# A long convolution and two gated layers on one core: second-batch loads behind the words that are read, weight pieces decoded in halves, first weights loaded behind the last chunk

## The chip, the cores and the metric

The kernel runs on one core of one Trainium2 chip. The metric is the device time of one execution in microseconds (us). The core has a matrix engine (PE, TensorE), VectorE (DVE), ScalarE (ACT), GpSimd (POOL), and a queue (SP, SyncE) that issues all of this kernel's DMAs, which 16 DMA engines carry out.

## What is computed

Two batches of 3008 tokens with 256 channels pass a convolution over the whole sequence (by Fourier transform), and then two layers on each token. The first gates by silu and is 1536 wide, the second gates by a hard swish and is 2048 wide.

```
X = np.fft.rfft(x, axis=1)
Y = X * (filt_r + 1j * filt_i)[None, :, :]
y = np.fft.irfft(Y, n=x.shape[1], axis=1)         # (2, 3008, 256)
g = x @ w_gate; silu = g / (1 + exp(-g))          # x: y as 6016 tokens; 256 -> 1536
x = silu * (x @ w_val) @ w_out                    # 1536 -> 256
h = x @ w_in                                      # 256 -> 2048
out = (h * clip(h + 3, 0, 6) / 6) @ w_out2        # 2048 -> 256
```

The weights are float64. The kernel reads them as pairs of 32-bit words and makes a float32 value of each pair (it *decodes* them); that value is then split into a high and a low part for the matmuls.

## The kernel before

**Prologue.** The sequence of 3008 is 47 x 64, and the transform is made in two stages. Stage one of batch 0 (`time_to_slots`) makes 32 frequency slots and stores them to memory (`d1`). The **chunk stage** (lines 539 to 572, `i` from 0 to 18) then goes over 17 chunks of one or two slots. PE multiplies chunk `i` (L543); VectorE multiplies it with the filter (`filter_product`: L198, L200, L201, and a sum L149, which POOL does and for the last three chunks VectorE); two rounds later PE transforms back (`back`, L524), ScalarE copies the result to `qall` (L525), and SP stores a part of it to `d2` (L526). SP loads chunk `i + 4` (L460) and its filter (L469). The last two chunks (15 and 16) also go straight into the first block: `straight` (L535) multiplies them with the matrix `direct`, which is loaded into `late_mat`. The other slots come back from `d2` into `near` (`load_near`, L515): 16 slots, then 13, for the first block (`near[:, :4]`), and later all 32 for the second (`near[:, 4:]`).

**Weights.** `Decode` loads raw words (L243) and decodes in three parts: `start` (ScalarE's absolute value, L248), `leading` (VectorE, three instructions on the high word, L256, L257, L259) and `rest` (L266, L267 on the low word, and an add, L149, on POOL unless VectorE is named). `word` is `leading` and `rest`. `parts_w1` splits the result: ScalarE casts the high part, POOL makes the difference (L146). The first layer's weights come in 12 pieces `f` of 128 hidden units. The first two are loaded apart: gate and value parts by `load_gv` (words in `side`), the output parts of both as `both`. From piece 2 on `decode_w1` uses two places in `x0` in turn. The two places of `load_gv`'s words in `side` overlap: `side[:, 2560:3584]` holds the words of piece 1 and also the first two units of the second batch (`x1_unit`, loaded by `load_x1`, L502).

**Main loop** (from line 672). A step `t` multiplies one block of 512 tokens with one piece: gate and value, 12 matmuls (`l1`, L310). ScalarE's silu (L729) and VectorE's product (L751) make the hidden values `h`. Two steps are a pair `p`. In the first 12 pairs blocks 0 and 1 are taken in turn, so steps 0 to 3 use pieces 0 and 1, steps 4 to 7 pieces 2 and 3, steps 8 to 11 pieces 4 and 5. In each odd step PE also runs layer two of the pair before (`l2_plain`, 12 matmuls, L158); for that, ScalarE casts `h` to `hs` (L153) and VectorE makes its low part (L146). Step 1 also transforms `near[:, 4:]` into `xsd[1]` (L224), and a step of a pair brings units of the second batch through stage one (`staged`, L165).

The order of instructions on each engine is that of the program. SP keeps eight DMAs under way: each one that it issues waits until the one eight places before it has landed.

Of the kernel before, what the change touches and what calls it, by code (L numbers as in the profile page):

```python
# [20 lines left out]
NS = 32  # L21
# [6 lines left out]
DIRECT = 3  # L28
# [85 lines left out]
def fft_conv_glu_mlp(ctx: ExitStack, tc: tile.TileContext, x, filt, mats, direct, sgn, w1, w2, out):  # L114
    nc = tc.nc
    w1, w2 = w1.bitcast(U32), w2.bitcast(U32)
    n_chunk = len(CHUNKS)
# [24 lines left out]
    def bank(tag="gv"):  # L142
        return ps.tile([P, 512], F32, tag=tag, name=tag)
# [28 lines left out]
    def alone(i):  # L172

        return int(i == 0)
# [5 lines left out]
    def prepare_filter(i, ft, by_slot=False, both=True, top=0):  # L180

        s0, n = CHUNKS[i]
        o = slice(top, top + 64)
        if both:
            nc.scalar.copy(out=ft[64 - top:128 - top, :n, 0], in_=ft[o, :n, 0])
        if by_slot:
            for r in range(n):
                nc.scalar.mul(out=ft[o, r, 1], in_=ft[o, r, 1], mul=sg[o, s0 + r:s0 + r + 1])
            return
        nc.gpsimd.tensor_tensor(out=ft[o, :n, 1], in0=ft[o, :n, 1],  # L190
                                in1=sg[o, s0:s0 + n].unsqueeze(2).to_broadcast([64, n, D]), op=ALU.mult)

    def filter_product(i, acc, ft, u, t2, engine=nc.gpsimd, top=0):

        n = CHUNKS[i][1]
        o = slice(top, top + 64)
        xa = acc[:, :n * D].rearrange("p (s c) -> p s c", c=D)
        nc.vector.scalar_tensor_tensor(out=t2[0:64, :n], in0=xa[64:128], scalar=-1.0, in1=ft[o, :n, 1],  # L198
                                       op0=ALU.mult, op1=ALU.mult)
        nc.vector.tensor_tensor(out=t2[64:128, :n], in0=xa[0:64], in1=ft[o, :n, 1], op=ALU.mult)  # L200
        nc.vector.tensor_tensor(out=u[:, :n], in0=xa, in1=ft[:, :n, 0], op=ALU.mult)  # L201
        plus(u[:, :n], u[:, :n], t2[:, :n], engine)
        return u.rearrange("p s c -> p (s c)")[:, :n * D]
# [70 lines left out]
    def decode_w1(f):  # L274
        a = x0[:, f % 2 * 3072:][:, :3072]
        return Decode(None, w1[:, f, :], 768, (words(a[:, :1536]), a[:, 1536:2304], a[:, 2304:]))
# [9 lines left out]
    def parts_w1(d, f, engine=nc.gpsimd):  # L286
        parts_gv(d, f, engine)
        parts_o1(d, f, engine)
# [14 lines left out]
    def ntok(k):  # L303
        return BLOCKS[blocks[k][1]][1] * N2
# [112 lines left out]
    with tc.manual_schedule():  # L417
# [30 lines left out]
        def idle(n, cols):  # L448

            acc = bank()  # L450
            for _ in range(n):
                nc.tensor.matmul(acc[:, :cols], mat[:, 0, :], mat.rearrange("p a c -> p (a c)")[:, :cols])
# [4 lines left out]
        def load_chunk(i):  # L457
            s0, n = CHUNKS[i]
            bts[i] = x0[:96, 4096 + i % 4 * 512:][:, :n * D]
            nc.sync.dma_start(out=bts[i].rearrange("p (s c) -> p s c", c=D), in_=rows(d1[0], s0, n))  # L460

        def top(i):

            return i % 2 * 64

        def load_filter(i):
            s0, n = CHUNKS[i]
            fts[i] = x0[:, i % 4 * 1024:][:, :n * 2 * D].rearrange("p (s r c) -> p s r c", r=2, c=D)
            nc.sync.dma_start(out=fts[i][top(i):top(i) + N1P], in_=filt[0:N1P, s0:s0 + n])  # L469
# [9 lines left out]
        def words(a):  # L479
            return a.bitcast(U32).rearrange("p (n t) -> p n t", t=2)  # L480

        dec = {}

        def load_gv(f):
            a = (new_y if f == 0 else lambda: work.tile([P, 1024], F32, tag="g", name="g", bufs=1))()
            dec[f] = Decode(None, w1[:, f, :1024], 512, (words(side[:, 2560 * f:][:, :1024]), a[:, :512], a[:, 512:]))
# [14 lines left out]
        def load_x1(u):  # L501
            nc.sync.dma_start(out=x1_unit(u), in_=x[1, :, u * 512:(u + 1) * 512])  # L502
# [8 lines left out]
        def load_near(a, b, k=0):  # L511

            m = slice(4 * k, 4 * k + 4)
            for r in range(a, P, NS):
                nc.sync.dma_start(out=near[r:r + b - a, m],  # L515
                                  in_=d2[0].rearrange("m p c -> p m c")[r:r + b - a, m])
# [3 lines left out]
        def back(q):  # L520

            s0, n = CHUNKS[q]
            acc = bank("a")
            nc.tensor.matmul(acc[:96, :n * D], mat[:, 3 + alone(q), :96], ys[q])  # L524
            nc.scalar.copy(out=qall[:96, s0 * D:(s0 + n) * D], in_=acc[:96, :n * D])  # L525
            nc.sync.dma_start(out=rows(d2[0], s0, n)[0:32], in_=qs[0:32, s0:s0 + n])  # L526

        def straight(q):

            s0, n = CHUNKS[q]  # L530
            if not sums:
                sums.extend([bank("a"), bank("a")])
            for a in range(2):
                for r in range(n):
                    nc.tensor.matmul(sums[a], ys[q][:, r * D + a * P:r * D + (a + 1) * P],  # L535
                                     late_mat[:, s0 + r - NS + DIRECT],
                                     start=s0 + r == NS - DIRECT, stop=False)

        for i in range(n_chunk + 2):
            if i < n_chunk:  # L540
                n = CHUNKS[i][1]
                acc = bank()
                nc.tensor.matmul(acc[:, :n * D], mat[:96, 1 + alone(i), :], bts.pop(i))  # L543
                if i < 4:
                    idle(1, 384)
                if i % 2 == 0:
                    us = mlp.tile([P, 2, 2, 2, D], F32, tag="h", name="us")
                ys[i] = filter_product(i, acc, fts.pop(i), us[:, 0, i % 2], us[:, 1, i % 2],
                                       nc.vector if i >= n_chunk - 3 else nc.gpsimd, top(i))
                if i + 4 < n_chunk:  # L550
                    load_chunk(i + 4)
                    load_filter(i + 4)
                if i in (7, 10):
                    load_gv(i // 10)
                if i == 12:
                    nc.sync.dma_start(out=late_mat, in_=direct)
            if i in (n_chunk - 2, n_chunk - 1):
                dec[i - n_chunk + 2].start()
            q = i - 2
            if 0 <= q < n_chunk - 2:  # L560
                back(q)
                del ys[q]
            if q == n_chunk - 2:
                straight(q)
                a = x0[:, 4608:]
                both = Decode(None, w1[:, 0:2, 1024:], 512, (words(a[:, :1024]), a[:, 1024:], dec[0].a))
                load_near(16, NS - DIRECT)
                for f in (2, 3):
                    dec[f] = decode_w1(f)
                both.start()  # L570
            if q == 11:
                load_near(0, 16)
            if i + 3 < n_chunk:
                prepare_filter(i + 3, fts[i + 3], i % 2 == 1 or i + 5 == n_chunk, top=top(i + 3))
        straight(n_chunk - 1)

        def high_gv(f):
            nc.scalar.copy(out=wgv[:, f, 0], in_=dec[f].w)  # L578
# [14 lines left out]
            back(q)  # L593
        ys.clear()
        load_near(0, NS, 1)
        for u in range(2):
            load_x1(u)
        dec[1].rest(nc.vector)
        high_gv(1)
        both.leading()  # L600
        low_gv(1)
# [70 lines left out]
        for t in range(2 * n_pair):  # L672
            p, i = divmod(t, 2)
            k, g_ = steps[p]
            n, f, c = ntok(k), 2 * g_ + i, p - FIRST
# [52 lines left out]
            h = hid[p].chunk(i)  # L728
            nc.scalar.activation(out=h, in_=hid[p].halves(gate), func=AF.Silu)  # L729

            d = 2 if t == 2 else p + 2 if i == 0 and p > 1 else None
            if d in dec:
                parts_w1(dec.pop(d), d)
            w = p + 3 if p and i == (p == 1) else None
            if t == 1:
                for r in range(2):
                    nc.scalar.copy(out=xsd[1][:, 0, r], in_=second_block[r])
# [1 line left out]
                    store_slots(1, 2 * u, staged(u, "a"))  # L739
            if t in (0, 1):  # L740
                dec[t + 2].start()
            if w in dec and t != 3:
                dec[w].start()
            if 1 <= p < 10 and i == 1:
                for u in (p + 1,) if p < 2 else (3, 4) if p == 2 else (p + 2,):
# [27 lines left out]
            if t == 3:  # L773
                dec[3].rest(nc.vector)
                parts_w1(dec.pop(3), 3)
                dec[5] = decode_w1(5)
                dec[4].start()
            if half:
                split_time(xsd[after[0]], *half)
            if i == 1 and (p == 0 or g_ == G1 - 1 and 0 < k < n_block - 2):  # L780
# [4 lines left out]
            if conv and i == 0:  # L785
                conv_store(c - 2)
                conv_split_in(c + 1)
                conv_load(c + 2)
            if w in dec:
                dec[w].word()  # L790
                if w + 2 < F1:
                    dec[w + 2] = decode_w1(w + 2)
            if 0 < p < 9 and i == 0:
# [23 lines left out]
            if base is not None and t >= base:  # L817
                q, r = divmod(t - base, 4)
                if q < G2:
# [8 lines left out]
                    elif r == 3:  # L828
                        w = late[q].w.rearrange("p (s c) -> p s c", c=P)
# [156 lines left out]
```

## Time and profile before

| | before |
|---|---|
| median of 3 runs | 1232.26 us (1231.95 to 1232.35) |
| the profiled execution, its span | 1232.27 us, 1230.5 us |
| PE busy | 1195.6 us, 97% of the span |
| VectorE busy | 1070.7 us, 87% |
| ScalarE, POOL busy | 640.3 us (52%), 147.0 us (12%) |
| granted PE clock, first four slices of 31 us | 1.00, 1.00, 0.83, 0.89; from then on 0.9 or more |
| chain of waits by engine | PE 60%, VectorE 33%, DMA 3% |
| mean of ScalarE's silu (L729), VectorE's product (L751) | 0.59 us, 0.67 us |

Busy time says where an engine works, not what sets the end. For that the chain of waits is read: it goes back from the last instruction to what released each step. The granted clock has two levels, 1.0 for 2.4 GHz and 0.5 for 1.2 GHz.

### The profile page before, as it was taken

What the parts mean: (1) busy time and instruction counts of PE and PEld (TensorE: products, weight loads), DVE (VectorE), ACT (ScalarE), POOL (GpSimd) and SP (SyncE); (2) the same over time, 40 slices, a digit from 0 to 9 for tenths busy, and PEclk for the clock granted to TensorE, in tenths of its full rate; (3) what the DMA queues carried; (4) which work ended last, traced back from release to release, by engine and by line L of the source; (5) the groups of instructions that cost most, each with busy time, mean ns of one, the idle gap of its engine ahead of it and who ended that gap; (6) DMA issues with size and microseconds to landing.
All of it is one profiled execution on the core that took longest, in us unless ns stands there. A gap on an engine that the chain in (4) does not pass through costs nothing.

```text
span 1230.5 us, 17678 instructions
## 1 busy us (share of the span) xinstructions
PE 1195.6 (97%) x6758; PEld 1028.7 (84%) x6758; DVE 1070.7 (87%) x1654; ACT 640.3 (52%) x990; POOL 147.0 (12%) x122
## 2 busy tenths in 40 slices
PE   8869999999999999999999999999999999999997
PEld 4246777888889988888888989989999999899997
DVE  1867768999997888877887899999999999999998
ACT  3634445555544444344444555555655565565554
POOL 2604440000000222211122320000000000000000
PEclk9988999999999999999999999999999999999999
DMA  9855423333302222121110310110011101101100
GB/s 287 222 195 186 139 86 119 85 110 93 102 21 72 82 80 99 48 70 35 55 66 16 121 51 1 35 36 35 1 33 35 33 1 35 35 1 35 33 18 15
DMA packets 46279, 86.82 MB, mean 71 GB/s; under 512 B 4852, under 2 KB 23748, under 8 KB 46068
## 3 DMA queue, kind: packets, MB, share of 16 engines
q1 hardware_dynamic: 46196, 85.71, 22.3%
q8 instruction: 53, 0.87, 0.3%
q14 instruction: 30, 0.25, 0.1%
HBM read 57.11 MB, written 28.57 MB: 70 GB/s over the span
## 4 chain that ended last, share of the span: by engine, by line
PE 60%; DVE 33%; DMA 3%; issue 2%; ACT 1%; SPq 0%; POOL 0%; DVEq 0%; ACTq 0%; POOLq 0%
PE gv L310 35%; PE a L319 16%; DVE hs L146 11%; DVE h L924 7%; DVE h L146 7%; PE a L158 3%; DVE h L149 3%; PE gv L158 2%; DMA x<-filt_in 1%; PE gv L224 1%; DVE y L391 1%; DVE y L146 1%; PE gv L165 1%; DVE xs L146 1%; DMA d<-qall 1%
## 5 line engine op out<-in xcount | busy, mean ns | idle before, releaser
L310 PE MATMUL gv<-xs,wall 128*128 128x512 f32 (+1 forms) x1728 | 416.0, 394 | 9.3 <-ACT wall L578 7.4
L319 PEld LDWEIGHTS a<-hs,wall 128*128 128x128 f32 x3276 | 408.6, 189 | 13.8 <-ACT hs L368 1.1
L319 PE MATMUL a<-hs,wall 128*128 128x256 f32 (+1 forms) x3276 | 416.2, 282 | 2.2 <-ACT hs L368 0.9
L310 PEld LDWEIGHTS gv<-xs,wall 128*128 128x128 f32 x1728 | 322.3, 189 | 78.9 <-ACT wall L578 7.9
L146 DVE TENSOR_TENSOR hs<-h,hs 128x768 fp32r<-128x768 f32 (+2 forms) x324 | 349.5, 1079 | 32.7 <-ACT hs L153 16.4
L310 PE MATMUL gv<-xs,wi 128*128 128x512 f32 (+1 forms) x1152 | 275.9, 388 | 0.0
L361 ACT CAST hs<-h 128x768 fp32r<-128x768 f32 (+1 forms) x156 | 128.1, 821 | 264.8 <-DVE h L924 159.4
L310 PEld LDWEIGHTS gv<-xs,wi 128*128 128x128 f32 x1152 | 210.0, 188 | 37.1 <-DVE xs L146 0.4
L368 ACT CAST hs<-h 128x1024 fp32r<-128x1024 f32 (+1 forms) x156 | 160.8, 1030 | 63.3 <-DVE h L146 63.3
L146 DVE TENSOR_TENSOR h<-h 128x512 f32<-128x512 f32 (+3 forms) x312 | 182.6, 585 | 8.7
L924 DVE SCALAR_TENSOR_TENSOR h<-h,gv 128x512 f32<-128x512 f32 (+1 forms) x192 | 128.2, 668 | 0.0
L751 DVE TENSOR_TENSOR h<-h,gv 128x512 f32<-128x512 f32 (+1 forms) x144 | 96.5, 670 | 34.2 <-PE gv L310 32.2
L729 ACT ACTIVATE h<-gv 128x512 f32<-128x512 f32 (+1 forms) x144 | 84.5, 587 | 63.9 <-PE gv L310 63.6
L920 ACT ACTIVATE h<-gv 128x512 f32<-128x512 f32 (+1 forms) x192 | 111.7, 582 | 0.9 <-PE gv L310 0.9
L149 DVE TENSOR_TENSOR h<-h 128x256 f32<-128x256 f32 (+1 forms) x156 | 68.1, 436 | 5.3
L149 POOL TENSOR_TENSOR ww<-ww,wa 128x512 f32<-128x512 f32 x16 | 20.7, 1294 | 394.2 <-DVE wa L267 394.2
L158 PE MATMUL a<-hs,wall 128*128 128x512 f32 x144 | 38.2, 417 | 3.5 <-DVE hs L146 3.5
L158 PEld LDWEIGHTS a<-hs,wall 128*128 128x128 f32 x144 | 28.5, 200 | 11.0 <-DVE hs L146 4.4
L198 DVE SCALAR_TENSOR_TENSOR us<-gv,x 64x512 f32<-64x512 f32 (+1 forms) x17 | 11.3, 662 | 28.9 <-PE gv L543 26.0
L146 POOL TENSOR_TENSOR wall<-x,wall 128x512 fp32r<-128x512 f32 (+1 forms) x20 | 23.8, 1212 | 55.7 <-ACT wall L153 55.7
L153 ACT CAST xs<-gv 128x512 fp32r<-128x512 f32 (+1 forms) x20 | 11.5, 576 | 33.7 <-PE gv L224 33.7
L146 DVE TENSOR_TENSOR y<-y,p 128x256 f32<-128x256 f32 (+3 forms) x44 | 24.9, 567 | 3.0
(130 smaller groups left out, 775.1 us busy)
## 6 DMA issues: line engine op xcount, KB each, us to landing
raw<-w_in SPq DMA_DIRECT2D x16, 512.0 KB, 4.5
x<-w_in SPq DMA_DIRECT2D x10, 768.0 KB, 5.0
g<-d SPq DMA_DIRECT2D x10, 512.0 KB, 4.2
yd<-y SPq DMA_DIRECT2D x10, 512.0 KB, 2.9
g<-yd SPq DMA_DIRECT2D x10, 512.0 KB, 3.8
y_out<-y SPq DMA_DIRECT2D x20, 256.0 KB, 2.3
ft<-filt_in SPq DMA_DIRECT2D x15, 256.0 KB, 3.6
wt<-wd SPq DMA_DIRECT2D x8, 448.0 KB, 3.2
```

The lines of the kernel that those rows point to most:

```text
L146: (engine or nc.vector).tensor_tensor(out=out, in0=a, in1=b, op=ALU.subtract)
L149: (engine or nc.vector).tensor_tensor(out=out, in0=a, in1=b, op=ALU.add)
L158: nc.tensor.matmul(acc, w, v, start=first and i == 0, stop=last and i == 2)
L165: nc.tensor.matmul(acc, mat[:, 0, :], src)
L310: nc.tensor.matmul(acc[:, :n], w[:, r, k * P:(k + 1) * P], xs[:, v, k, :n], start=(r, v, k) == (0, 0, 0), stop=(r, k) == (1, 1))
L319: nc.tensor.matmul(acc[b][:, 256 * h:256 * h + nt], w[:, r, iw], hs[:, v, ih, :nt], start=first and h == 0 and v == 0 and r == 1, stop=las ...
L361: nc.scalar.copy(out=self.parts(0, 0, 3), in_=v(1, 4))
L368: nc.scalar.copy(out=self.parts(0, 3, 7), in_=self.values(4, 8))
L729: nc.scalar.activation(out=h, in_=hid[p].halves(gate), func=AF.Silu)
L751: nc.vector.tensor_tensor(out=h, in0=h, in1=hid[p].halves(val), op=ALU.mult)
L920: nc.scalar.activation(out=h, in_=pre, func=AF.Relu, bias=3.0)
L924: nc.vector.scalar_tensor_tensor(out=h, in0=h, scalar=6.0, in1=pre, op0=ALU.min, op1=ALU.mult)
```

## The change

- The two loads of the first weights (`load_gv`) move from rounds 7 and 10 of the chunk stage to rounds 12 and 13. In round 12 the last chunk has just been issued.
- Both absolute values of these pieces (`dec[f].start()`) move behind the last copy of chunk 14; the near loads move ahead of the load of `both`; the absolute value of `both` moves to behind `load_x1`.
- `dec[1].rest` moves ahead of `load_x1`: the loads of the second batch's first two units now overwrite the words after these have been read.
- Pieces 4 and 5 are started at steps 4 and 5, their `leading` and `rest` stand in two steps (4 and 5, 5 and 6) and the add is VectorE's. Piece 6 is started and decoded at step 7, with VectorE's add. Pieces from 7 on are as before.

```diff
-                if i in (7, 10):
-                    load_gv(i // 10)
+                if i in (12, 13):
+                    load_gv(i - 12)
...
-            if i in (n_chunk - 2, n_chunk - 1):
-                dec[i - n_chunk + 2].start()
...
             if q == n_chunk - 2:
+                for f in range(2):
+                    dec[f].start()
                 straight(q)
+                load_near(16, NS - DIRECT)
                 a = x0[:, 4608:]
                 both = Decode(None, w1[:, 0:2, 1024:], 512, (words(a[:, :1024]), a[:, 1024:], dec[0].a))
-                load_near(16, NS - DIRECT)
                 for f in (2, 3):
                     dec[f] = decode_w1(f)
-                both.start()
...
         load_near(0, NS, 1)
+        dec[1].rest(nc.vector)
         for u in range(2):
             load_x1(u)
-        dec[1].rest(nc.vector)
+        both.start()
         high_gv(1)
...
-            d = 2 if t == 2 else p + 2 if i == 0 and p > 1 else None
+            d = {2: 2, 6: 4, 7: 5}.get(t, p + 2 if i == 0 and p > 3 else None)
...
-            w = p + 3 if p and i == (p == 1) else None
+            w = {4: 4, 5: 5, 7: 6}.get(t, p + 3 if i == 0 and p > 3 else None)
...
-            if w in dec and t != 3:
+            if w in dec:
                 dec[w].start()
...
                 dec[5] = decode_w1(5)
-                dec[4].start()
+            if t == 4:
+                dec[4].leading()
+            if t in (5, 6):
+                dec[t - 1].rest(nc.vector)
+                dec[t + 1] = decode_w1(t + 1)
+            if t == 5:
+                dec[5].leading()
...
-            if w in dec:
-                dec[w].word()
+            if w in dec and w > 5:
+                dec[w].word(nc.vector if w == 6 else None)
```

SP at the end of the chunk stage. `side<-w_in` are the first weights, `side<-direct_in` the matrix of `straight`, `d_0_74<-qall` the stores of chunks 10 to 14, `x_102<-w_in` with 2x512 the load of `both`.

```order
 L469 DMA x_102<-filt_in 48x512
+L243 DMA side<-w_in 128x1024
 L556 DMA side<-direct_in 128x1536
-L526 DMA d_0_74<-qall 32x512 x2
+L526 DMA d_0_74<-qall 32x512
+L243 DMA side<-w_in 128x1024
+L526 DMA d_0_74<-qall 32x512
 L515 DMA near<-d_0_74 16x4x256 x4
 L526 DMA d_0_74<-qall 32x512 x3
+L515 DMA near<-d_0_74 13x4x256 x4
 L243 DMA x_102<-w_in 128x2x512
-L515 DMA near<-d_0_74 13x4x256 x4
```

The first weights now stand behind the last filter load and among the last stores; the third of the three stores is the eighth DMA behind the second weights load.

VectorE ahead of the main loop, with the semaphores that each waits for (DMAHW0 and DMAHW1 are here those of the two loads `side<-x_in`; `g` and `side` hold piece 1).

```order
 L266 TENSOR_SCALAR g<-g 128x512 [waits DVE_49]
-L267 SCALAR_TENSOR_TENSOR g<-side,g 128x512 [waits DMAHW1_49,DMAHW0_49,DVE_49]
+L267 SCALAR_TENSOR_TENSOR g<-side,g 128x512 [waits DVE_49]
 L149 TENSOR_TENSOR g<-g 128x512 [waits DVE_49]
-L256 TENSOR_SCALAR x_102<-x_102 128x512 [waits DMAHW4_49]
+L256 TENSOR_SCALAR x_102<-x_102 128x512 [waits Activation_49]
```

The order of the instructions is the same; the wait for the second batch's units is gone from L267.

VectorE at steps 3 to 5, where `hs` is what PE's layer two reads and the rows L256 to L267 decode a piece (`x_102`).

```order
 L267 SCALAR_TENSOR_TENSOR x_102<-x_102 128x768
 L149 TENSOR_TENSOR x_102<-x_102 128x768
+L146 TENSOR_TENSOR hs<-h,hs 128x1024
+L751 TENSOR_TENSOR h<-h,gv 128x512
+L256 TENSOR_SCALAR x_102<-x_102 128x768
+L257 TENSOR_SCALAR x_102<-x_102 128x768
+L259 SCALAR_TENSOR_TENSOR x_102<-x_102 128x768
+L751 TENSOR_TENSOR h<-h,gv 128x512
+L266 TENSOR_SCALAR x_102<-x_102 128x768
+L267 SCALAR_TENSOR_TENSOR x_102<-x_102 128x768
+L149 TENSOR_TENSOR x_102<-x_102 128x768
```

The first two rows end piece 3. Behind them now stands `hs` of pair 1, and piece 4 follows in two halves around the product of step 5; before, all of piece 4 stood ahead of that `hs`.

## Rows read from the trace of the kernel before

**Rows 1.** Waits of PE behind 116 us: engine, tile, line <- releaser: total, times, longest.
```profile
PE gv L310 <- ACT st L207: 1.8, 2, 0.9
```
**Rows 2.** Timeline, first wait: start, us, engine, line, operation, tiles, count [idle before <-releaser].
```profile
72.42 3.14 PE L310 MATMUL gv<-xs,wall 128*128 128x512 f32 x12
...
72.74 0.42 DVE L266 TENSOR_SCALAR g<-g 128x512 uint32<-128x512 uint32 x1
...
80.88 0.69 DVE L267 SCALAR_TENSOR_TENSOR g<-side,g 128x512 f32<-128x512 uint32 x1 [7.72 <-DMA side<-x_in]
...
83.00 5.49 PE L310 MATMUL gv<-xs,wall 128*128 128x512 f32 x12 [7.44 <-ACT wall L578]
...
88.29 2.02 PE L224 MATMUL a<-mat,near 128*128 128x128 f32 x16
...
90.97 1.29 DVE L146 TENSOR_TENSOR xs<-a,xs 128x512 fp32r<-128x512 f32 x2 [0.83 <-ACT xs L737]
...
91.47 6.13 PE L310 MATMUL gv<-xs,wall 128*128 128x512 f32 x24
```
**Rows 3.** Chain of waits, 73 to 81 us: start, us, what.
```profile
73.41 1.52 DMA d<-qall
...
77.25 3.51 DMA side<-x_in
```
**Rows 4.** Windows, 84 to 88 us: busy by engine, PE clock, DMA share, GB/s.
```profile
84.00:88.00 4.00, 4.00 (x11) 3.08 (x10) 3.86 (x8) 1.42 (x4) 0.00 (x0) 0.50 0.12 49
```
**Rows 5.** Timeline, second wait.
```profile
97.44 2.95 PE L158 MATMUL a<-hs,wall 128*128 128x512 f32 x12
...
101.52 0.96 DVE L149 TENSOR_TENSOR x<-x 128x768 f32<-128x768 f32 x1
...
102.52 0.93 ACT L153 CAST wall<-x 128x512 fp32r<-128x512 f32 x2 [0.65 <-DVE x L149]
...
104.15 1.04 ACT L153 CAST hs<-h 128x1024 fp32r<-128x1024 f32 x1
...
108.44 1.22 DVE L146 TENSOR_TENSOR hs<-h,hs 128x1024 fp32r<-128x1024 f32 x1
...
109.72 5.49 PE L158 MATMUL a<-hs,wall 128*128 128x512 f32 x12 [2.89 <-DVE hs L146]
```
**Rows 6.** Chunk stage: timeline of chunks 1, 8 and 14; chain; SP's waits; weights load.
```profile
26.43 0.69 DVE L198 SCALAR_TENSOR_TENSOR us<-gv,x 64x512 f32<-64x512 f32 x1 [0.57 <-issue]
...
41.84 0.69 DVE L198 SCALAR_TENSOR_TENSOR us<-gv,x 64x512 f32<-64x512 f32 x1
...
57.49 0.69 DVE L198 SCALAR_TENSOR_TENSOR us<-gv,x 64x512 f32<-64x512 f32 x1 [0.82 <-PE gv L543]
...
46.15 6.61 DMA x<-filt_in
...
SPq L460 <- DMA side<-w_in: 1.2, 1, 1.2
...
side<-w_in SPq DMA_DIRECT2D x2, 512.0 KB, 6.2
```
**Rows 7.** From the last chunks to the near rows: timeline and chain.
```profile
63.27 5.39 PE L535 MATMUL a<-side,us 128*128 128x512 f32 x12 [1.74 <-ACT qall L525]
...
63.30 1.58 DMA d<-qall
...
66.21 3.11 DMA near<-d
...
69.46 2.02 PE L224 MATMUL a<-mat,near 128*128 128x128 f32 x16 [0.80 <-DMA near<-d]
```
**Rows 8.** Timeline: a piece's first instruction alone and beside POOL's differences.
```profile
86.73 0.55 DVE L256 TENSOR_SCALAR x<-x 128x768 f32<-128x768 f32 x1
...
95.48 2.53 POOL L146 TENSOR_TENSOR wall<-x,wall 128x512 fp32r<-128x512 f32 x2 [37.48 <-ACT wall L153]
...
96.36 1.06 DVE L256 TENSOR_SCALAR x<-x 128x768 f32<-128x768 f32 x1
```

## The prediction, made before the changed kernel ran

> **What bounds the kernel now.** The chain of waits comes first: 60% of the span on PE and 33% on VectorE, in one long tail that starts at about 117 us. The list of PE's waits behind that point holds nothing longer than the two waits of 0.9 us of [rows 1], so from there the kernel is a belt that runs at its own pace: whatever is won or lost ahead of it moves the end by the same amount. The question is when the belt starts. I then read the timeline of the first 117 us for PE, and behind each gap the row that ended it.
>
> Three places stand out. First, PE runs twelve matmuls of the main loop at 72.42, and then idles for 7.44 us until 83.00 [rows 2]. The row names ScalarE's cast of the second weight piece; that cast waits for VectorE, whose L267 waits for the DMA side<-x_in, landed at 80.8 [rows 2, 3]. L267 reads words of a weight; x_in is the second batch. It waits because the program writes those loads ahead of it, into the same place. Behind the gap the granted clock is 0.50, the 1.2 GHz level, and the next twelve matmuls take 5.49 us where the twelve ahead of it took 3.14 [rows 2, 4]. Second, at 109.72 PE has idled 2.89 us for hs, and again runs at half pace: 5.49 us where the same group took 2.95 [rows 5]. Third, the chunk stage slows: VectorE takes 15.41 us from chunk 1 to chunk 8, 2.20 each, but 15.65 us for the six to chunk 14 [rows 6]; there one filter load takes 6.61 us, and SP holds a chunk's load for 1.2 us until the first weights load has landed.
>
> **The change part by part.** *Weights behind the last chunk.* Two 512 KB loads leave the stretch from 43 to 53 us. At the old pace six chunks take 13.2 us, so up to 15.65 - 13.2 = 2.45 us come back; the lower bound is 0, if the chunks' own traffic sets the pace. But the loads now stand, with the 768 KB of `direct`, behind the last chunk and ahead of the stores and near loads. What follows is PE's straight block, 63.27 plus 5.39 us [rows 7], and then the near rows, which PE awaited for 0.80 us until 69.46. Moving ScalarE's two absolute values behind the copies frees the last copy about a microsecond earlier, before the near loads leave. Against that, a store waits for the load eight places before it on SP (the 1.2 us of [rows 6] is such a wait): in the new order this is the second weights load for the last early store. I put its issue at about 55, and such a load took 6.2 us [rows 6], so the store leaves near 61.2 instead of 63.3 [rows 7]: 2.1 us earlier. With the load of `both` no longer ahead of the near rows (they took 3.11 us) a little more. The straight block allows at most 2.45 + 0.80 = 3.25. I take **2.5 us**, nearest to the store's bound; ends 0 and 3.25.
>
> The load of `both` now stands behind four near loads. VectorE first needs it after the second piece, the old 82.3, now about 72; its cover is the near rows' transform and the first twelve matmuls, some 5 us. I cost it at nothing; without that cover it is four near issues, at most the 2.3 us between 74.93 and 77.25 in which four such stand [rows 3].
>
> *Units of the second batch after the words are read.* L267 then starts when VectorE has ended L266, at 73.16 (72.74 + 0.42) instead of 80.88 [rows 2]. The wait of 7.44 us goes, and with it the half clock: 5.49 - 3.14 = 2.35. What is late next? PE alone would reach the 24 matmuls of 91.47 like this: 72.42 less 2.5 is 69.9; two groups of 3.14 end at 76.2; the near transform and two units take 91.47 - 88.29 = 3.18, so 79.4. VectorE has a solid row of work from L267 to the end of the two xs differences: 80.88 to 90.97 + 1.29 = 92.26, 11.38 us, of which 0.83 was a wait for ScalarE that an earlier PE removes. From 73.16 - 2.5 = 70.7 it ends at 81.2. PE's fourth matmul wants the second difference, three matmuls of 0.26 us after its start, so PE starts at 80.4. VectorE is the bound, by 1 us. The near rows of the second batch were issued behind a store that lands at 74.93, and land before side<-x_in does at 80.76 [rows 3]; moved by 2.5 they come between 74.0 (74.93 + 1.52, as long as a store takes) and 78.3. PE asks at 76.2. They are issued ahead of side<-x_in, whose part of the chain begins at 77.25, so I take them as landed by about 76; at 78.3 PE would start at 81.5, 1.1 us later. Net: 91.47 to 80.4 is 11.1, less the 2.5 counted already: **8.6 us**; ends 7.5 and 9.8 (7.44 + 2.35).
>
> *Pieces four to six.* VectorE ended piece three at 101.52 + 0.96 = 102.5 and then did the whole of piece four ahead of hs, which started at 108.44 [rows 5]. Now hs stands directly behind piece three: ScalarE's two casts of the piece (0.93) and of hs (1.04) end at 104.5, VectorE's 1.22 at 105.7. PE asked at 109.72 - 2.89 = 106.8, and both are moved about alike, so it has 1.1 us in hand. The wait and its half clock go: 2.89 + (5.49 - 2.95) = 5.43. The adds of pieces four to six leave POOL for VectorE: 3 times 0.96 us [rows 5]. Queued behind them are the hs of steps 7 and 9, and behind those PE. For step 7 the halves are spread and VectorE is some 2 us early. For step 9: behind step 7's matmuls PE has its layer-two group and 24 matmuls, 2.95 + 6.13 = 9.1 us [rows 2, 5]. VectorE waits for ScalarE's silu (0.6), multiplies (0.68), waits for piece six's start behind piece five's casts (about 1.1), decodes it on its own in at most 5.4 (piece three took 96.36 to 102.48 with a product of 0.68 inside, [rows 5, 8]) and makes hs in 1.22: 9.0 to 9.6. So up to 0.5 us late; with other small waits I take 0.6. Net **4.8 us**; ends 0 and 5.43. POOL loses work only, and SP's later piece loads keep their place behind the pieces that they replace.
>
> Here a rule is to be weighed. Beside POOL's two differences (2.53 us), VectorE's L256 took 1.06 us instead of 0.55 [rows 8]. The Trainium skill (SBUF — State Buffer, section "SBUF: two separate sides") says more: VectorE and GpSimd share a port pair as an exclusive lock, the later one standing still until the other's instruction ends. By that, two differences could hold piece six for up to 2.53 us, some 1.6 more than the row's pace, and hs of step 9 would be about 2 us late. That is the second rival below; the row shows a partial delay.
>
> **Sum.** 2.5 + 8.6 + 4.8 = 15.9 us. The profiled execution took 1232.27 us (span 1230.5 and 1.8 around it), the median is 1232.26. 1232.3 - 15.9 = **1216.4 us**.
>
> **The rivals.** *The pile holds the store and the near rows.* 1.8 MB go out within some 2 us, and all that follows is in their queue. For: the 1.2 us that SP once stood behind a single weights load. Against: at 55 to 62 us the chunk loads are over. The first term is then 0: 1218.9.
>
> *VectorE is too full at steps 5 to 9*, once: hs is over 2 us late at step 9, PE idles as at 109.72 and runs at half clock after it. This gives back 5.4: 1221.8. For it: the 9.6 against 9.1 above. Against: the halves leave VectorE about 2 us early at step 7, so that it doesn't come to step 8 with arrears.
>
> *The first wait stays under another name*: the near rows or units land late and PE idles some 2 us in step 1 and loses the clock again (2.35): 8.6 becomes about 4.5, 1220.5.
>
> *Slower*: the adds on VectorE make hs late at every pair from step 7 on, not once. Each such time costs 5.4 as in [rows 5]; VectorE must lose more than PE's 2 us of slack per pair for four pairs in a row: 4 x 5.4 = 21.6 > 15.9, so 1238. From the third on (16.3) it decides: 1232.7 is no change. Against: from piece seven on the add is POOL's again, in the old order.
>
> **Chances.** Forecast 0.62, between 1213.0 and 1219.0. Pile 0.14, full VectorE once 0.11, first wait renamed 0.07, three late pairs 0.03, four 0.03. Best case: 3.25 + 9.8 + 5.43 = 18.5, 1213.8, and a little for unlisted slack: 1213.0. The range 1213.0 to 1222.0 takes in the first three rivals and leaves out under 0.2. A measurement tells 0.2%, about 2.5 us, from no change; the chances are 0.94 faster, 0.03 the same, 0.03 slower.
>
> **What would show it.** After the change, VectorE's L267 on side must follow L266 with no wait, and PE must have no gap over 1.5 us between about 70 and 120 us, with a granted clock of 1.0 throughout. PE's 24 matmuls of step 2 should start near 80.4; if VectorE is the bound, their wait is for xs from L146. The chunk 14 product should come at about 55 us. The group that stood at 109.72 should start some 14 to 16 us earlier and take 2.95. A gap at the near transform of step 1 would show the third rival, a wait for hs near 110 us the second. The forecast is wrong if PE loses its clock again anywhere in this stretch.

## The result and the profile after the change

| | before | after |
|---|---|---|
| median beside each other | 1231.95 us (1229.65 to 1232.35, 5 runs) | 1219.55 us (1219.01 to 1223.23, 5 runs) |
| the same once more, on another occasion | 1231.89 us (9 runs) | 1219.36 us (4 runs) |
| the profiled execution, its span | 1232.27, 1230.5 us | 1219.01, 1216.8 us |

The ratio is 0.991 (95% interval 0.9893 to 0.9928), the second time 0.9901 (0.9886 to 0.9915): 12.4 us faster, where 15.9 were forecast. The time lies in the range, which was drawn around the first three rivals; the part of it given to the forecast itself (1213.0 to 1219.0) it misses by 0.55 us. By its mechanism it is the first rival's (1218.9): the first term of the sum came to nothing that the runs show, the second was of the size forecast, and the third was smaller in the medians than in the sum.

**The first wait is gone.** The timeline of the changed kernel answers to [rows 2] (start, us, engine, line, operation, tiles, count, [idle before <-releaser]):

```profile
72.38 4.10 PE L310 MATMUL gv<-xs,wall 128*128 128x512 f32 x16
...
72.70 0.42 DVE L266 TENSOR_SCALAR g<-g 128x512 uint32<-128x512 uint32 x1
73.15 0.69 DVE L267 SCALAR_TENSOR_TENSOR g<-side,g 128x512 f32<-128x512 uint32 x1
...
76.75 2.12 PE L310 MATMUL gv<-xs,wall 128*128 128x512 f32 x8 [0.27 <-DVE wall L146]
79.52 2.02 PE L224 MATMUL a<-mat,near 128*128 128x128 f32 x16 [0.65 <-DMA near<-d]
...
82.33 1.28 DVE L146 TENSOR_TENSOR xs<-a,xs 128x512 fp32r<-128x512 f32 x2
...
82.70 6.15 PE L310 MATMUL gv<-xs,wall 128*128 128x512 f32 x24
```

L267 stands directly behind L266, without the 7.72 us of wait for side<-x_in. PE's 7.44 us have shrunk to 0.27 and 0.65, and step 2 starts at 82.70 instead of 91.47. VectorE's row from L267 to the end of xs now lasts 73.15 to 83.61, 10.46 us; the forecast had 10.55 (11.38 less the 0.83 of wait).

The order before did more than cost time. In `side` only the place of piece 1's words is shared with the two units, and both loads had landed there when L267 ran: it took bits of the second batch for the low words of piece 1. L267 scales a low word by 2^-52, so that each of these weights was off by less than 2^-20 of its power of two. The moved line removes a wait and a read of wrong words.

**The second wait is gone, and a small new one stands four steps behind it.** The timeline answers to [rows 5]; the layer-two groups L158 of steps 5 and 9, and some of VectorE's row ahead of them:

```profile
95.79 1.23 DVE L146 TENSOR_TENSOR hs<-h,hs 128x1024 fp32r<-128x1024 f32 x1 [1.95 <-ACT hs L153]
...
97.92 2.96 PE L158 MATMUL a<-hs,wall 128*128 128x512 f32 x12
...
106.57 1.06 DVE L266 TENSOR_SCALAR x<-x 128x768 uint32<-128x768 uint32 x1
107.66 1.38 DVE L267 SCALAR_TENSOR_TENSOR x<-x 128x768 f32<-128x768 uint32 x1
...
111.84 0.62 DVE L256 TENSOR_SCALAR x<-x 128x768 f32<-128x768 f32 x1 [1.21 <-ACT x L248]
...
118.24 3.07 PE L158 MATMUL a<-hs,wall 128*128 128x512 f32 x12 [0.81 <-DVE hs L146]
```

At step 5 VectorE is now so early that it waits 1.95 us for ScalarE's cast; PE doesn't wait, and the group takes 2.96 us where it took 5.49. At step 9 PE waits 0.81 us for hs. Ahead of it VectorE stood 1.21 us, until ScalarE had started piece 6.

**The clock.** Windows of the changed kernel: busy time of PE, PEld, DVE, ACT, POOL, then granted PE clock, DMA share, GB/s. They answer to [rows 4]:

```profile
56.00:62.00 6.00, 4.13 (x11) 1.48 (x10) 5.80 (x9) 4.94 (x10) 1.27 (x1) 1.00 0.99 347
62.00:66.00 4.00, 4.00 (x6) 1.60 (x6) 3.80 (x9) 0.68 (x1) 0.00 (x0) 0.57 0.38 66
...
70.00:84.00 14.00, 13.08 (x65) 9.49 (x65) 12.32 (x22) 8.00 (x16) 0.00 (x0) 1.00 0.87 331
84.00:96.00 12.00, 12.00 (x51) 9.29 (x50) 9.85 (x13) 6.34 (x11) 4.00 (x4) 1.00 0.92 292
96.00:108.00 12.00, 12.00 (x49) 9.09 (x49) 11.62 (x16) 6.48 (x11) 4.32 (x3) 1.00 0.52 179
108.00:125.00 17.00, 16.19 (x66) 12.16 (x65) 14.18 (x17) 7.60 (x13) 6.52 (x6) 1.00 0.43 131
```

From 70 to 125 us the clock is 1.00 throughout. At 62 to 66 us it is 0.57, mostly the 1.2 GHz level, where the straight block runs; in [rows 7] the block took 5.39 us, and here 7.08.

**The loads bring nothing that shows.** Timeline of chunks 8 and 14 and of what follows them, the chain of waits (start, us, what), and a wait of SP's (total, times, longest); they answer to [rows 6, 7]:

```profile
43.13 0.69 DVE L198 SCALAR_TENSOR_TENSOR us<-gv,x 64x512 f32<-64x512 f32 x1
56.02 0.69 DVE L198 SCALAR_TENSOR_TENSOR us<-gv,x 64x512 f32<-64x512 f32 x1
...
61.80 7.08 PE L535 MATMUL a<-side,us 128*128 128x512 f32 x12 [1.74 <-DVE us L149]
69.42 2.02 PE L224 MATMUL a<-mat,near 128*128 128x128 f32 x16 [0.54 <-DMA near<-d]
...
55.95 7.84 DMA side<-w_in
...
63.85 1.59 DMA d<-qall
...
66.77 2.40 DMA near<-d
...
SPq L526 <- DMA side<-w_in: 1.8, 1, 1.8
```

The six chunks take 12.89 us instead of 15.65, so the straight block starts 1.47 us earlier than in [rows 7] (the chunks before had been 1.3 us later in this execution). But the near transform starts at 69.42, and at 69.46 before. What ends last are the near rows: SP holds the last early stores 1.8 us until the second weights load has landed at 63.79, so the store leaves at 63.85 (63.30 before), the near rows land behind it, and PE waits 0.54 us for them. Close ahead of that the straight block ends, at 68.88, since it runs at the low clock, 7.08 us instead of 5.39; by itself it would have left 0.6 us of the gain.

### The profile page after: what moved, and what is told of

Its sections match the earlier page's. It is cut to its first block, busy times and chain, and to the rows that moved or that the text cites. A ratio compares the mean times of both kernels' runs of the same rounds, so it can differ in the third digit from the quotient of the medians.

```text
span 1216.8 us, 17683 instructions
## 1 busy us (share of the span) xinstructions
PE 1194.2 (98%) x6758; PEld 1026.1 (84%) x6758; DVE 1073.9 (88%) x1657; ACT 641.2 (53%) x990; POOL 142.7 (12%) x119
## 4 chain that ended last, share of the span: by engine, by line
PE 56%; DVE 38%; issue 3%; DMA 2%; ACT 1%; POOL 0%; SPq 0%; DVEq 0%; ACTq 0%; POOLq 0%
PE gv L310 32%; PE a L319 15%; DVE hs L146 13%; DVE h L930 8%; DVE h L146 7%; DVE h L149 3%; PE a L158 2%; PE gv L158 2%; PE gv L224 1%; DVE y L391 1%; DVE y L146 1%; DVE xs L146 1%; PE gv L452 1%; PE gv L165 1%; DMA side<-w_in 1%
## 5 line engine op out<-in xcount | busy, mean ns | idle before, releaser
L751 DVE TENSOR_TENSOR h<-h,gv 128x512 f32<-128x512 f32 (+1 forms) x144 | 96.7, 671 | 34.1 <-PE gv L310 31.2
L158 PE MATMUL a<-hs,wall 128*128 128x512 f32 x144 | 35.8, 397 | 1.4 <-DVE hs L146 1.4
L158 PEld LDWEIGHTS a<-hs,wall 128*128 128x128 f32 x144 | 26.9, 188 | 8.5 <-DVE hs L146 2.3
```

Of the source, the lines that this page charges most:

```text
L158: nc.tensor.matmul(acc, w, v, start=first and i == 0, stop=last and i == 2)
L751: nc.vector.tensor_tensor(out=h, in0=h, in1=hid[p].halves(val), op=ALU.mult)
```

## The experiments

**Each part alone, and the other two together** (the first four ran beside the same runs of the kernel before: 1232.08 us, 23 runs).

*The units alone:* the kernel before with

```diff
+        dec[1].rest(nc.vector)
         for u in range(2):
             load_x1(u)
-        dec[1].rest(nc.vector)
```

> The kernel before with one edit: the rest of piece 1 stands ahead of the loads of the second batch's first units. Theory (the wait and its half clock are this term alone; the moved weight loads add nothing): the 24 matmuls of step 2 start 8.5 to 9 us earlier than at 91.47, and as the wait for hs at step 5 stays, the time is about 1223.3. Rival (part of the 8.75 us that step 2 gained in the changed kernel came from the moved loads): 7 us or less, 1225 or more.

Measured: 1223.58 us, ratio 0.9934 (0.9917 to 0.9951), 8.5 us less. Its timeline shows step 2 started as in the changed kernel, and the second wait untouched, with a part of the clock's loss:

```profile
82.17 6.14 PE L310 MATMUL gv<-xs,wall 128*128 128x512 f32 x24
...
100.48 4.60 PE L158 MATMUL a<-hs,wall 128*128 128x512 f32 x12 [2.92 <-DVE hs L146]
```

*The pieces alone:* the kernel before with the changed lines of the main loop (pieces four and five in halves, piece six at step 7, their adds on VectorE).

> The kernel before with one edit: pieces 4 to 6 started, halved and added as in the changed kernel. Theory: the wait of 2.89 us for hs and its half clock go, about 0.8 us come back at step 9 as in the changed kernel: 4.9 us less, 1227.1. Rival (the second wait is a consequence of the first one, whose late VectorE work it inherits): VectorE is still late at step 5 and under 2 us are won, 1230 or more.

Measured: 1229.38 us, 0.9975 (0.9964 to 0.9986), 2.7 us less (1.7 to 4.4): between the two theories, nearer to the rival's 1230. The rival's cause isn't it, though: at step 5 PE waits for nothing in this profile.

```profile
106.91 2.96 PE L158 MATMUL a<-hs,wall 128*128 128x512 f32 x12
```

*The loads alone:* the kernel before with the changed lines of the chunk stage, and with the absolute value of `both` behind `load_x1`.

> The kernel before with one edit: first weights behind the last chunk, their absolute values and the load of both as in the changed kernel. Theory: the chunk stage runs 2.5 us faster behind chunk 8, but the last early store waits for the second weights load, which takes about 7.8 us, so the near transform starts no earlier than 69: 0 to 1 us less, 1231 to 1232. Rival (the forecast's first term holds, and only a late prologue hid it in the profile): 2.5 us less, 1229.5.

Measured: 1231.81 us, 1.0001 (0.9989 to 1.0014): nothing that shows between 1.4 us less and 1.7 us more. In this profile the straight block keeps its clock, and PE waits 1.03 us for the near rows all the same; the store ahead of them leaves at 61.68, behind a second weights load of 6.34 us. The profile also gives a reason for the pieces' 2.7 us: the second wait is as long here as in [rows 5], but no clock is lost behind it (timeline, and a window with the granted clock third from the end):

```profile
61.15 5.39 PE L535 MATMUL a<-side,us 128*128 128x512 f32 x12 [1.74 <-DVE us L149]
...
67.56 2.02 PE L224 MATMUL a<-mat,near 128*128 128x128 f32 x16 [1.03 <-DMA near<-d]
...
107.89 3.05 PE L158 MATMUL a<-hs,wall 128*128 128x512 f32 x12 [2.87 <-DVE hs L146]
...
100.00:112.00 12.00, 9.13 (x37) 6.68 (x36) 7.05 (x9) 5.62 (x11) 6.73 (x5) 1.00 0.49 153
```

A wait of 2.87 us is followed by 3.05 us of matmuls here, and one of 2.89 by 5.49 in [rows 5]. In the four profiles that keep this wait (2.87 to 3.02 us) the group behind it took 5.49, 4.60, 3.05 and 3.06 us. The 2.5 us of the low clock are not in every execution, and a part that removes the wait saves them only where they are.

*Units and pieces, the loads as before:*

> The changed kernel with the first weights loaded in rounds 7 and 10 as before, absolute values and near loads too: the two other edits together. Theory (the moved loads are worth nothing on the whole): within 1 us of the changed kernel, 1218.5 to 1219.5. Rival (they are worth 2.5 us): 2 to 2.5 us slower than the changed kernel, 1221.5 to 1222.

Measured: 1220.07 us, 0.9909 (0.9891 to 0.9927), the changed kernel's ratio. So beside the other parts, too, the loads bring nothing that the intervals show.

The table sets stretches of the profiled executions side by side, in us, each a difference of two starts in the timelines. They leave out the prologue, which alone differs by a microsecond and more between executions.

| kernel | chunk 8 to 14 | chunk 16 to near transform | near transform to L158 of step 3 | L158, step 3 to step 9 |
|---|---|---|---|---|
| before | 15.65 | 6.26 | 27.98 | 34.46 |
| units alone | 14.61 | 6.71 | 19.32 | 33.29 |
| pieces alone | 14.99 | 6.20 | 27.19 | 29.42 |
| loads alone | 12.82 | 6.48 | 28.06 | 32.71 |
| units and pieces | 14.59 | 6.79 | 19.25 | 29.58 |
| changed | 12.89 | 7.69 | 19.27 | 29.55 |
| changed, again | 16.22 | 7.20 | 19.24 | 29.59 |

The third column is the units' (8.7 us less wherever they are), the fourth the pieces' (3.1 to 5.0 less, by the clock of the other kernel). The first column is the loads': with them moved as in the changed kernel the six chunks took 12.81 to 12.89 us in four of five profiles, and with the loads as before 14.59 to 17.31 in five (the runs further down included). It isn't sure, though: the changed kernel's second profile took 16.22. And what the chunks win is mostly lost in the second column.

**The changed kernel again.**

> The changed kernel itself, run again beside the three variants below so that they can be compared on one chip. It was 0.991 of the kernel before (0.9893 to 0.9928), 1219.6 us. Expected of both theories: 0.990 to 0.992 again, 1219 to 1220.5 us.

Measured: 1219.36 us, 0.9901. In its chunk stage the filter loads are late with no weights beside them. Waits between 46 and 56 us (waiting engine, tile, line <- releaser: total, times, longest):

```profile
ACT x L185 <- DMA x<-filt_in: 3.7, 3, 1.7
```

Here the near rows end no wait: the low clock of the straight block does, and the near transform follows it at once (timeline):

```profile
63.59 7.08 PE L535 MATMUL a<-side,us 128*128 128x512 f32 x12 [1.74 <-DVE us L149]
70.72 2.02 PE L224 MATMUL a<-mat,near 128*128 128x128 f32 x16
```

**Can the loads' gain be kept?** The changed kernel with the second weights load behind the near loads, so that it holds no store:

```diff
-                if i in (12, 13):
-                    load_gv(i - 12)
+                if i == 12:
+                    load_gv(0)
...
                 load_near(16, NS - DIRECT)
+                load_gv(1)
```

(`start` and `leading` of that piece move behind `low_gv(0)`.)

> The changed kernel with the second weights load moved behind the 13-slot near loads, and its absolute value and first half behind the first piece's difference. Theory (the last early store was held to 63.8 us only by the eighth DMA ahead of it, the second weights load): the store leaves at about 61, the near rows are there by 67, and the near transform starts as soon as the straight block ends, at 67.2 if the clock is kept there and 68.9 if not: 0.5 to 2 us less than the changed kernel, 1217.5 to 1219. Rival (the near rows are late for another reason, the traffic of all the loads): the near transform still waits until 69, and the time is that of the changed kernel, 1219.5.

> The variant with the second weights' load behind the near rows, run again, with more rounds than the first time and on the same chip as the changed kernel. Theory: the near rows' stores are no longer held by that load, worth 0.3 to 0.8 us: 1218.8 to 1219.2 us where the changed kernel takes 1219.6. Rival: what the near rows win, VectorE's wait for the second weights (1.63 us in the earlier profile) takes back in full: within 0.2 us of the changed kernel.

Measured: 1218.83 us, 0.9887 (0.9874 to 0.9901); again, 1218.12 us, 0.9893 (0.9877 to 0.9909), beside 0.9901 of the changed kernel. Timeline of the first, with a wait of SP's from it:

```profile
68.72 1.95 PE L224 MATMUL a<-mat,near 128*128 128x128 f32 x16
...
69.92 0.43 DVE L256 TENSOR_SCALAR g<-g 128x512 f32<-128x512 f32 x1 [1.63 <-ACT g L248]
...
81.91 6.87 PE L310 MATMUL gv<-xs,wall 128*128 128x512 f32 x24
...
SPq L526 <- DMA side<-direct_in: 1.5, 1, 1.5
```

And of the second:

```profile
60.93 5.39 PE L535 MATMUL a<-side,us 128*128 128x512 f32 x12 [1.74 <-DVE us L149]
66.65 2.02 PE L224 MATMUL a<-mat,near 128*128 128x128 f32 x16 [0.34 <-DMA near<-d]
```

In the first the transform follows the straight block at once, in the second, where the block keeps its clock, after 0.34 us. A store is still held, now by `direct`, which stands eight places ahead of it (1.5 us, in the second profile 1.0). And VectorE stands 1.63 us (1.65) for the second weights, which SP issues behind the near rows. From chunk 16 to step 3's L158 both profiles of this variant take 26.90 us, and the changed kernel 26.96 and 26.44: what the near rows won, the weights take back. The medians are 0.7 us (not beside the changed kernel; by the ratios 2.8) and 1.2 us lower all the same, with intervals that overlap the changed kernel's; where these come from no profile here shows.

*The clock of the straight block kept* (the same variant, with three matmuls of 320 columns for nothing ahead of it):

```diff
                 dec[0].start()
+                idle(3, 320)
                 straight(q)
```

> The kernel of e5 with three idle fp32 matmuls of 320 columns ahead of the straight block, in the 1.74 us in which PE waits for VectorE there (the result is not used). Theory (the half clock at 62 to 65 us, which made the straight block 7.08 us long instead of 5.39, comes from that gap): the block takes 5.39 and the near transform starts 1.7 us earlier than in e5 where e5 lost its clock; 1217 to 1217.5. Rival (the clock falls there whatever fills the gap, or the near rows are the later of the two): as e5.

Measured: 1218.88 us, 0.9895 (0.988 to 0.9911), no less than without. Timeline:

```profile
65.16 5.39 PE L535 MATMUL a<-side,us 128*128 128x512 f32 x12 [0.86 <-DMA side<-direct_in]
...
75.71 4.24 PE L310 MATMUL gv<-xs,wall 128*128 128x512 f32 x14 [0.79 <-DVE xs L146]
```

The block runs at full clock, but in this profile it waits for its own matrix (`direct`) until 65.16, and PE later waits 0.79 us for VectorE, so it doesn't price the clock by itself. The two profiles above do: with the block at 7.08 us and at 5.39 the stretch to step 3 takes the same 26.90 us. In this variant the low clock of that block is no bound of its own.

**What is the first wait's clock worth?** The kernel before with eleven matmuls of 384 columns for nothing inside its first wait.

> The kernel before with eleven idle fp32 matmuls of 384 columns (7.1 us, result not used) in PE's first wait, so that the wait stays and the clock doesn't fall. It prices the half clock behind the first wait by itself. Theory (VectorE is the bound behind the wait, and so hides most of the 2.35 us that the twelve matmuls lose): the matmuls of step 1 take 3.14, the 24 of step 2 start at 90.6 instead of 91.47, 0.9 us less, 1231.2. Rival (PE is the bound there): the whole 2.35 come back, 1229.7.

Measured: 1231.75 us, 0.9987 (0.9976 to 0.9998), 1.4 us less than 1233.13 (0.2 to 3.0): between theory (0.9) and rival (2.35), and the time excludes neither. In the profile the stretch from the near transform to step 3's layer two takes 27.04 us where it took 27.98: 0.94 less, the theory's. Timeline:

```profile
77.50 7.26 PE L690 MATMUL a<-mat 128*128 128x384 f32 x22
...
92.28 1.28 DVE L146 TENSOR_TENSOR xs<-a,xs 128x512 fp32r<-128x512 f32 x2
...
93.02 5.75 PE L310 MATMUL gv<-xs,wall 128*128 128x512 f32 x22 [0.21 <-DVE xs L146]
```

With the clock at 1.00, PE is held by VectorE's xs in the middle of step 2, as the prediction said that VectorE is the bound behind this wait. What is left of the low clock's 2.35 then lies under VectorE's row.

**Who ends the wait at step 9?** The adds of pieces four to six back on POOL:

> The changed kernel with the adds of pieces 4 to 6 back on POOL; the halves stay. Theory (VectorE's row of work is what ends the 0.81 us wait for hs at step 9): VectorE does 2.9 us less between steps 5 and 8, the wait at step 9 goes and the time is 0.8 us less, 1218.7. Rival (the adds are on POOL late, behind its differences): the casts of pieces 5 and 6 wait for POOL, PE waits for a piece's low part at step 9 or 12, 1219.5 or more.

Measured: 1221.89 us, 0.9915 (0.9901 to 0.9928): nothing won. It comes out 0.6 us (by the ratios, whose intervals overlap) to 2.3 us (by medians not taken beside each other) above the changed kernel; in its profile step 11's L158 comes 41.4 us behind step 3's, in the changed kernel's 38.9. The theory that VectorE's three adds (0.96 each) make the wait falls. Timeline:

```profile
101.35 2.03 POOL L149 TENSOR_TENSOR x<-x 128x768 f32<-128x768 f32 x1 [4.33 <-DVE x L267]
101.78 2.02 DVE L257 TENSOR_SCALAR x<-x 128x768 uint32<-128x768 uint32 x1
...
111.25 0.93 ACT L153 CAST wall<-x 128x512 fp32r<-128x512 f32 x2 [4.29 <-POOL x L149]
...
113.02 0.63 DVE L256 TENSOR_SCALAR x<-x 128x768 f32<-128x768 f32 x1 [3.49 <-ACT x L248]
...
118.44 1.89 PE L158 MATMUL a<-hs,wall 128*128 128x512 f32 x7 [1.49 <-DVE hs L146]
```

POOL's add takes 1.83 to 2.76 us instead of VectorE's 0.96, ScalarE's casts of the piece wait for it, piece 6 is started behind the casts, and VectorE waits 3.49 us for that start. The chain add, casts, start decides, not VectorE's load.

So the start goes ahead of the casts:

```diff
+            if t == 7 and w in dec:
+                dec[w].start()
             if d in dec:
                 parts_w1(dec.pop(d), d)
```

> The changed kernel with one instruction moved: at step 7 ScalarE's start of piece 6 (0.91 us) stands ahead of its two casts of piece 5 (0.93 us together) instead of behind them. Theory: the last loss in the belt, 0.81 us before step 9's layer-two block, hangs on that start, since VectorE waits 1.21 us for it at 111.84 us and every later step of piece 6 follows; with the start 0.9 us earlier VectorE's wait falls from 1.21 to about 0.3 us, the split for step 9 is done 0.9 us earlier and the wait is gone: 0.8 us less than the changed kernel, 1218.7 us. Rival: the casts of piece 5, now 0.9 us later, are what ends next (ScalarE's row is as long as before, and TensorE's layer-one block of step 8 needs piece 5's tile), so a wait of 0.3 to 0.9 us appears there, and the time stays within 0.3 us of the changed kernel's.

Measured: 1218.71 us, 0.9899 (0.9882 to 0.9917), 0.65 us below the changed kernel beside it, with overlapping intervals. Timeline:

```profile
110.23 0.55 DVE L256 TENSOR_SCALAR x<-x 128x768 f32<-128x768 f32 x1
...
110.45 2.49 POOL L146 TENSOR_TENSOR wall<-x,wall 128x512 fp32r<-128x512 f32 x2 [2.54 <-ACT wall L153]
110.89 1.45 DVE L257 TENSOR_SCALAR x<-x 128x768 uint32<-128x768 uint32 x1
112.37 1.38 DVE L259 SCALAR_TENSOR_TENSOR x<-x 128x768 uint32<-128x768 uint32 x1
...
117.53 3.07 PE L158 MATMUL a<-hs,wall 128*128 128x512 f32 x12 [0.47 <-DVE hs L146]
```

VectorE's wait of 1.21 us is gone, but PE's falls only from 0.81 to 0.47: piece 6 now begins beside POOL's differences of piece 5, where L257 and L259 take 1.45 and 1.38 us; in the changed kernel they took 0.92 and 0.96. That is 0.95 of the 1.21 given back.

*Both edits, weights last and piece 6 first:*

> Both edits: the second weights' load behind the near rows, and piece 6 started ahead of piece 5's casts. Theory: the first takes some 0.7 us before the first step in those executions where the near rows' wait ends last (it ran at 1218.8 against 1219.6 us before), the second 0.8 us at step 9, and they don't meet: 1217.5 to 1218.3 us, faster than both kernels. Rival: VectorE's row behind the second weights gives the first back and piece 5's casts give the second back: 1219 to 1219.6 us.

Measured: 1218.01 us (1216.87 to 1219.21), 0.9888 (0.9871 to 0.9906): the lowest median of all, 1.35 us under the changed kernel beside it, but not told apart from it with certainty, since the intervals overlap.

## Why the prediction came out as it did

- **The bound: right.** The start of step 9's L158 lies 1098.6 us before the end of the span in both kernels (1230.5 - 131.90 and 1216.8 - 118.24). All of the change happens ahead of it, as the reading of [rows 1] had it.
- **The first wait, 8.6 us: right in mechanism and size.** Its sign, step 2 near 80.4, came at 82.70, later by about the first term that is missing. From the near transform to step 3's layer two it is 27.98 - 19.27 = 8.7 us, and 8.5 us in the time when this part is made alone. The low clock's 2.35 were rightly not added in full; filling the wait brought 1.4 in the time and 0.94 in the profile. The loads of the near rows for the second batch came a little late (0.65), inside the bounds given. The moved load of `both` cost nothing: VectorE's first instruction on it, at 74.49, follows the row ahead without a wait.
- **The pieces, 4.8 us: right for the profiled execution (34.46 - 29.55 = 4.9), too much for the median.** Alone they bring 2.7 us, with the units 3.5 (1223.58 to 1220.07). The step that failed is "the wait and its half clock go": the 2.5 us of half clock were read from one execution as if each had them. Over the four profiles that keep the wait the loss is 1.1 us on average, and 2.9 + 1.1 - 0.8 = 3.2 us (an estimate from these rows) lies between the 2.7 and the 3.5. The lateness at step 9 was forecast as 0.6 and is 0.81.
- **The weights behind the last chunk, 2.5 us: wrong; no run tells it from 0,** the lower end and the first rival. The gain in the chunk stage itself came in four of five profiles, though the weights beside the chunks aren't their only brake: the second profile of the changed kernel has the slow pace without them. The steps that failed lie behind the chunks. The last early store was to leave near 61.2; it left at 63.85, because the load that holds it was issued at 55.95 and not at 55, and took 7.84 us and not the 6.2 of [rows 6]. Between 56 and 62 us the DMA engines are 99% busy (70% in the kernel before) with the loads that now stand together; that the chunk loads are over by then, the argument against the rival, doesn't touch this. In the four profiles of this order whose chain of waits goes through that load it took 6.34 to 8.11 us. The straight block was taken as 5.39 us and came at 7.04 to 7.08 in five of the eight profiles with the moved loads and no filling (in none of the five with the loads as before). What is left is small: over five profiles of this order the near transform starts at 69.12 us on average (67.56 to 70.72), over five with the loads as before at 70.12 (68.83 to 71.57), so that a gain of about a microsecond isn't excluded.
- **The second rival** was weighed with a rule of the Trainium skill (SBUF — State Buffer, section "SBUF: two separate sides"): VectorE and GpSimd share a pair of ports as an exclusive lock, which a VectorE instruction in a two-port mode or with two inputs in SBUF needs as well as GpSimd's, and the later one stands until the other's instruction ends. The prediction read [rows 8] as a partial delay against that rule, and feared 1.6 us beyond the row's pace. That reading was wrong; the rows agree with the rule. POOL's two differences at step 7 of the changed kernel:

```profile
105.30 1.91 POOL L146 TENSOR_TENSOR wall<-x,wall 128x512 fp32r<-128x512 f32 x1 [7.68 <-ACT wall L153]
107.17 1.05 POOL L146 TENSOR_TENSOR wall<-x,wall 128x256 fp32r<-128x256 f32 x1
```

  They end at 107.21 and 108.22. L266 and L267, which take 0.55 and 0.96 us alone, end at 107.63 and 109.04 (the rows under the second wait): each 0.13 to 0.14 ahead of the end of one POOL instruction plus its own time. So VectorE loses what is left of one POOL instruction at a time, here 0.93 us for both, and the rival's two microseconds at step 9 didn't come. The 2.02 us of L257 beside POOL's add of 2.03 fit in the same way: 103.38 + 0.56 against 103.80.
- **The slower case** had no sign in the traces: behind step 9 PE waits nowhere longer than 0.9 us, and the longest wait of layer two for VectorE's hs there is 0.6.

## What to carry to other kernels

A transfer that is written ahead of the last reader of its place puts its own landing into that reader's way, and the reader then gets the new words; moving the reader's three instructions ahead of it was two thirds of the gain, and a single moved line. A load that is moved out of one busy stretch has to be followed into the next one: count what it stands ahead of in the queue, and which issue waits for its landing. What a low clock costs behind a wait should be read from more than one execution before it goes into a sum.

## What the runs showed of the hardware

- The granted clock doesn't follow from the length of the idle time ahead. Ahead of the straight block PE idled 1.74 us in the kernel before and ran 5.39 us; the changed kernel idled 1.74 us and took 7.08. Waits of 2.89 and 2.87 us were followed by 5.49 and 3.05 us for the same matmuls. What decides it stays open.
- VectorE and POOL hold each other up by whole instructions. In both kernels, between 84 and 132 us, each VectorE instruction that POOL delayed ended 0.13 to 0.15 us ahead of POOL's end plus its own time alone. The product L751, which reads the matmul's result, kept its 0.68 us beside POOL. POOL waits in its turn: in the run with the adds on POOL an undisturbed add of 128x768 values took 1.83 us, and one that began inside VectorE's difference of 1.22 us (117.17 to 118.39) took 2.76; 118.39 + 1.83 is 0.13 more than its end at 120.09.
- A load of 512 KB that was issued into full DMA engines (347 GB/s from 56 to 62 us) took 7.84 us. The engines stayed full until 63 us, while only 139 GB/s moved in the last of these microseconds, and it landed at 63.79, when they were 21% busy.
